# Last rows of w_out and an eighth of one wo group moved to partitions 0 to 31, and O picked in two operations, in a decode block that streams its KV cache

## The chip, the cores and the metric

One core of a Trainium2 chip. The metric is the device time of one execution in microseconds; lower is better. Times inside a profile are counted from the start of its span.

## The reference, cut to what matters

```python
x = A_x                                    # 4 rows of 640, bf16
xn = layernorm(x)
# A: q = xn @ wq (32 heads of 128); attention over k_cache, v_cache (4, 32, 4096, 128); @ wo (4096 x 640)
# B: z = gelu(xn @ w_in); z1 * (w_sp * layernorm(z2) + b_sp) @ w_out (864 x 640)
return x + A(xn) + B(xn)
```

The two caches are 268 MB of the 282 MB that the kernel reads. Each of them is walked in 16 units of 8 MB, named K0 to K15 and V0 to V15; four units, one for each batch row, make a group of eight heads.

## The kernel before

A unit of 128 partitions x 64 KB lies in two of the five slots of one large buffer, so at most two units and a half are there at once. The order is K0 to K3, then V0, K4, V1, K5 and so on. All weights pass through the same five slots.

```python
SL = T * Dh // 2
kv = const.tile([P, 5 * SL], BF16)
def at_slot(i, n, off=0):
    return kv[:, i * SL + off:i * SL + off + n]
...
nc.sync.dma_start(out=w_out[:, 0:FC - 1, :], in_=B_w_out[0:nf, :].rearrange("(p c) n -> p c n", p=P))
nc.sync.dma_start(out=w_out[:FL, FC - 1, :], in_=B_w_out[nf:Fh, :])        # the last 96 rows
...
cuts = {("k", u): (0, T // 2, T) for u in range(NU) if u % B == B - 1}     # K3, K7, K11, K15 in two loads
wo_t = [at_slot((4, 0, 1, 2)[g], HG * NOUT).rearrange("p (c n) -> p c n", c=HG) for g in range(NG)]
...
def emit_K(u, k):                     # eight times for each K unit
    kw = unit(("k", u), t0, t0 + 2 * TC)...
    kT = ktpool.tile([P, 2 * TC * 32], F32, tag="kT", name="kT")          # two buffers
    nc.vector.transpose(kT[:].rearrange("p (t r) -> p t r", r=32), kw)
    ...                               # then 8 matmuls into S
...
# in emit_V: picking O, four operations of 128 elements
nc.vector.tensor_scalar(out=R, in0=O_ps[:, 0, :], scalar1=Mk4[:, 0:1], scalar2=None, op0=ALU.mult)
for c in range(1, 4):
    nc.vector.scalar_tensor_tensor(out=R, in0=O_ps[:, c, :], scalar=Mk4[:, c:c + 1], in1=R, op0=ALU.mult, op1=ALU.add)
...
# in the main loop: the next unit is loaded while this one is computed
load_unit(seq[i + 1])
if key == "k" and u == 2 * B - 1:     # behind both halves of K7
    load_wo(u // B - 1)               # the first wo group, 128 rows of 10 KB, into slot 4
```

Of the kernel before, what the change touches and what calls it, by code (L numbers as in the profile page):

```python
# [16 lines left out]
def kernel(  # L17
# [36 lines left out]
    G = HG * B  # L54
    F2 = B_w_in.shape[1]
    Fh = F2 // 2
    FC = (Fh + P - 1) // P
    FL = Fh - (FC - 1) * P
    NOUT = A_wo.shape[1]
    NH = 2  # L60
    NO2 = NOUT // NH
# [29 lines left out]


    n_q = DC * H * Dh
    wq = at_slot(0, n_q).rearrange("p (c n) -> p c n", c=DC)
    nc.sync.dma_start(out=wq, in_=A_wq.rearrange("(p c) n -> p c n", c=DC))

    ln_t = at_slot(0, 8 * D, n_q)
    x_bf = ln_t[:B, 0:D]
    nc.scalar.dma_start(out=x_bf, in_=x_flat)

    x_res = const.tile([32, NO2], BF16)
    nc.vector.memset(x_res[:], 0.0)

    n_in = DC * F2
    w_in = at_slot(2, n_in).rearrange("p (c f) -> p c f", c=DC)
    nc.sync.dma_start(out=w_in, in_=B_w_in.rearrange("(p c) f -> p c f", c=DC))
    w_out = at_slot(2, FC * NOUT, n_in).rearrange("p (c n) -> p c n", c=FC)

    nf = (FC - 1) * P
    nc.sync.dma_start(out=w_out[:, 0:FC - 1, :], in_=B_w_out[0:nf, :].rearrange("(p c) n -> p c n", p=P))  # L110
    nc.sync.dma_start(out=w_out[:FL, FC - 1, :], in_=B_w_out[nf:Fh, :])  # L111
    sb_bf = const.tile([1, 2], BF16)
    nc.sync.dma_start(out=sb_bf[:, 0:1], in_=B_w_sp)
    nc.sync.dma_start(out=sb_bf[:, 1:2], in_=B_b_sp[None, :])


    seq = [("k", u) for u in range(B)]
# [34 lines left out]

    wo_q = A_wo.rearrange("(g p c) n -> g p c n", p=P, c=HG)
    wo_t = [at_slot((4, 0, 1, 2)[g], HG * NOUT).rearrange("p (c n) -> p c n", c=HG) for g in range(NG)]

    def load_wo(g, c_cuts=(0, HG)):
        for c0, c1 in zip(c_cuts[:-1], c_cuts[1:]):
# [117 lines left out]
    zT_ps = misc_ps([P, 2, FC, B], F32)  # L275
    for part in range(2):
        for fc in range(FC):
            n = P if fc < FC - 1 else FL
            f0 = part * Fh
            for c in range(DC):  # L280
                if fc < FC - 1:
                    w = w_in[:, c, f0:f0 + nf].rearrange("p (f a) -> p a f", a=FC - 1)[:, fc, :]
                else:
                    w = w_in[:, c, f0 + nf:f0 + Fh]
                nc.tensor.matmul(zT_ps[:n, part, fc, :], lhsT=w,
                                 rhs=xnT[:, c, 0:B], start=(c == 0), stop=(c == DC - 1))
    zT = const.tile([P, 2, FC, B], F32)
    nc.vector.memset(zT[:], 0.0)
    uT = const.tile([P, FC, 32], BF16)
    nc.vector.memset(uT[:], 0.0)  # L290
    nc.scalar.activation(out=zT[:, :, 0:FC - 1, :], in_=zT_ps[:, :, 0:FC - 1, :], func=ACT.Gelu_apprx_tanh)
    nc.scalar.activation(out=zT[:FL, :, FC - 1, :], in_=zT_ps[:FL, :, FC - 1, :], func=ACT.Gelu_apprx_tanh)

    one_bf = const.tile([1, P], BF16)
    nc.vector.memset(one_bf[:], 1.0)
# [36 lines left out]


    for fc in range(FC):
        n = P if fc < FC - 1 else FL
        nb = B if fc > 1 else 32
        r0 = 64 * (fc % 2)
        for hf in range(NH):
            nc.tensor.matmul(proj[r0 + 32 * hf:r0 + 32 * hf + nb, 0:NO2], lhsT=uT[:n, fc, 0:nb],
                             rhs=w_out[:n, fc, hf * NO2:(hf + 1) * NO2], start=(fc < 2), stop=False)  # L340


    def fill_qz(g):
# [92 lines left out]
    def emit_V(v):  # L436
        g, b = divmod(v, B)
        O_ps = ps_o.tile([P, 4, Dh], F32, tag="O", name="O")
        vv = unit(("v", v), 0, T)
        for w in range(NW):  # L440
            q = w % 4
            nc.tensor.matmul(O_ps[32 * q:32 * q + 32, :, :], lhsT=Zb[b % 2][:, w].rearrange("p h c -> p (h c)"),  # L442
                             rhs=vv[:, w * 4 * Dh:(w + 1) * 4 * Dh], start=(w < 4), stop=(w >= NW - 4))

        if b == 0:
            R_new = small.tile([P, B, Dh], F32, tag="R", name="R", bufs=1)
            state["R"] = R_new
        R = state["R"][:, b, :]
        nc.vector.tensor_scalar(out=R, in0=O_ps[:, 0, :], scalar1=Mk4[:, 0:1], scalar2=None, op0=ALU.mult)  # L449
        for c in range(1, 4):  # L450
            nc.vector.scalar_tensor_tensor(out=R, in0=O_ps[:, c, :], scalar=Mk4[:, c:c + 1], in1=R, op0=ALU.mult, op1=ALU.add)  # L451
        if b + 2 < B:
            z_fill(g, b + 2)

# [11 lines left out]

    def emit_oT(g):
        om = state.pop(("om", g))[:].rearrange("p h (q c) -> p c h q", c=HG)
        oT_ps = misc_ps([P, HG, B], F32)
        for c in range(HG):  # L470
            nc.tensor.matmul(oT_ps[:, c, :], lhsT=om[:, c, :, :], rhs=B32[:], start=True, stop=True)
        oT = small.tile([P, HG, B], BF16, tag="oT", bufs=3)
        nc.vector.tensor_copy(out=oT[:], in_=oT_ps[:])
        state[("oT", g)] = oT

    def emit_proj(g, cs=range(HG)):
        oT = state[("oT", g)]
        for c in cs:
            for hf in range(NH):
                r0 = 64 * (c % 2) + 32 * hf  # L480
                nc.tensor.matmul(proj[r0:r0 + B, 0:NO2], lhsT=oT[:, c, :],
                                 rhs=wo_t[g][:, c, hf * NO2:(hf + 1) * NO2],
                                 start=False, stop=(g == NG - 2 and c >= HG - 2))

    fill_qz(0)
    for i, item in enumerate(seq):
        if i + 1 < len(seq):
            key, u = seq[i + 1]
            if u == NU - 2 and key == "v":
                x_rows = x_flat.rearrange("b (h n) -> (b h) n", h=NH)  # L490
                for r0, r1 in ((0, 3), (3, 2 * B)):
                    nc.sync.dma_start(out=x_res[4 * r0:4 * r1:4, :], in_=x_rows[r0:r1])
            load_unit(seq[i + 1])
            if key == "k" and u == 2 * B - 1:
                load_wo(u // B - 1)
        else:
            load_wo(NG - 3)
            load_wo(NG - 2)
            load_wo(NG - 1, (0, 4, 6, 7, 8))
        key, u = item  # L500
        g, b = divmod(u, B)
        if key == "k":
            done = b == B - 1 and g > 0
            for k in range(8):
                emit_K(u, k)
                if done and k == 1:
                    emit_sel(g - 1)
                if done and k == 2:
                    emit_oT(g - 1)
                if done and k == 5 and g == 1:  # L510
                    emit_proj(g - 1)
            if b == B - 1:
                if g < NG - 1:
                    fill_qz(g + 1)
                softmax(g)
        else:
            emit_V(u)
            if u == NU - 2:
                for hf in range(NH):
                    nc.tensor.matmul(proj[32 * hf:32 * hf + B, 0:NO2], lhsT=ident_bf[:32, 4 * hf:32:8], rhs=x_res[:],  # L520
                                     start=False, stop=False)
# [10 lines left out]
    oT = state[("oT", NG - 1)]  # L532
    for c in range(HG):

        lhsT = oT[:].rearrange("p c b -> p (c b)") if c == 0 else oT[:, c, :]
        for hf in range(NH):
            nc.tensor.matmul(last[32 * hf:32 * hf + (32 if c == 0 else B), :], lhsT=lhsT,  # L537
                             rhs=wo_t[NG - 1][:, c, hf * NO2:(hf + 1) * NO2], start=(c == 0), stop=(c == HG - 1))
# [33 lines left out]
```

## Time and profile before

| | before |
|---|---|
| median of 3 runs | 665.3 us (664.97 to 665.37) |
| span of the profiled run | 663.5 us |
| main load queue, share of 16 DMA engines' span | 98.8% |
| busiest compute engine | VectorE 54% |
| K7's transposes begin | 247.62 and 257.44 us |
| K8 issued, V5 issued | 266.40, 287.30 us |
| last data landed | 659.93 us |

Three things in the profile carry the argument. The *DMA row* gives the mean busy share of the 16 DMA engines in each fortieth of the span. The *timeline* gives start, duration, engine, line and operation, then in brackets the idle time ahead and what ended it. And for each load the trace keeps its *completion writes*: 16 for a load of 128 rows, three and five for x_res's loads of three and five rows (one mark about 1 us after the issue, which these small loads have besides, is left out). I take each write for one DMA engine, so the engine that is ahead and the one that is behind can be told. The prediction below shows the lines.

### The profile page before, as it was taken

To read this page: it belongs to the slowest core of one execution; us is meant where nothing else is said; L and a number is where in the kernel's file an instruction comes from. 1 tells how busy PE (TensorE), PEld (TensorE's weight loads), DVE (VectorE), ACT (ScalarE), POOL (GpSimd) and SP (SyncE) were. 2 spreads that over 40 slices of the span, in tenths; PEclk is the share of its full clock that TensorE was granted. 3 is DMA by queue.
4 is the path that set the end of the run, shared out by engine and by line. 5 is a ranking of instruction groups with operands and counts; after the bars stand their busy time and mean duration, and the time that the engine had idled before them with its cause. 6 is when DMAs were issued, how large, how long until landed. Compare 5 with 4: busy or idle time off the path is not lost.

```text
span 663.5 us, 5584 instructions
## 1 busy us (share of the span) xinstructions
PE 298.7 (45%) x2366; PEld 111.7 (17%) x2366; DVE 359.9 (54%) x341; ACT 82.6 (12%) x169; POOL 6.2 (1%) x24
## 2 busy tenths in 40 slices
PE   0525765266073457235436075433607244624146
PEld 0401211022021122111112022111202112211012
DVE  5338999656190849509156286745628084940002
ACT  0300000440100000530200000070100000053200
POOL 0000000000000000000000000000000000000000
PEclk9758779678577786667758577865857778756777
DMA  9999999999999999999999999999999999999996
GB/s 368 457 439 420 409 441 440 439 436 436 423 431 440 419 426 448 435 432 423 436 439 432 431 423 438 437 440 435 416 435 436 443 435 412 444 423 436 426 419 248
DMA packets 6949, 282.61 MB, mean 426 GB/s; under 512 B 792, under 2 KB 1164, under 8 KB 1548
## 3 DMA queue, kind: packets, MB, share of 16 engines
q1 hardware_dynamic: 6908, 282.25, 98.8%
q8 instruction: 18, 0.29, 0.2%
q14 instruction: 7, 0.06, 0.0%
q10 hardware_dynamic: 16, 0.01, 0.0%
HBM read 282.25 MB, written 0.01 MB: 425 GB/s over the span
## 4 chain that ended last, share of the span: by engine, by line
DMA 73%; DVE 12%; issue 11%; PE 2%; ACT 1%; SPq 0%; DVEq 0%; ACTq 0%
DMA kv<-in_A_k_cache_dram 65%; DVE kT L360 11%; DMA kv<-in_A_v_cache_dram 4%; DMA kv<-in_A_wo_dram 3%; PE O L442 2%; DVE xd L425 0%; PE last L537 0%; ACT Zb L406 0%; ACT p L414 0%; DVE pT L418 0%; DVE m L378 0%; PE misc L383 0%; PE S L371 0%; SPq L111 0%; ACT xd L425 0%
## 5 line engine op out<-in xcount | busy, mean ns | idle before, releaser
L360 DVE STREAM_TRANSPOSE kT<-kv 128x2048 f32<-128x2048 f32 x128 | 282.8, 2275 | 126.1 <-DMA kv<-in_A_k_cache_dram 126.1
L371 PE MATMUL S<-kT,QZ 128*32 128x512 bf16 x1024 | 192.8, 511 | 230.4 <-DVE kT L360 230.4
L371 PEld LDWEIGHTS <-QZ 128*32 128x32 bf16 x1024 | 61.4, 112 | 355.6 <-issue 336.7
L442 PE MATMUL O<-kv,Zb 128*32 128x512 bf16 x1024 | 76.3, 464 | 59.7 <-ACT Zb L406 30.2
L449 DVE TENSOR_SCALAR R<-O,Mk 128x128 f32<-128x128 f32 x16 | 5.6, 351 | 129.8 <-PE O L442 129.8
L406 ACT ACTIVATE Zb<-xd,MkE 32x256 bf16<-32x256 bf16 x112 | 51.4, 498 | 106.0 <-PE O L442 104.6
L414 ACT ACTIVATE p<-S,negmax 128x512 bf16<-128x512 f32 x8 | 5.4, 683 | 400.4 <-DVE negmax L392 400.4
L442 PEld LDWEIGHTS <-Zb 128*32 128x32 bf16 x1024 | 33.1, 114 | 102.4 <-issue 58.3
L459 PE MATMUL misc<-R,SelR 128*32 128x128 f32 x32 | 6.4, 281 | 26.0 <-DVE R L451 26.0
L425 ACT COPY xd<-pT 32x256 bf16<-32x256 bf16 x28 | 17.2, 613 | 5.7 <-DVE pT L418 5.2
L451 DVE SCALAR_TENSOR_TENSOR R<-O,Mk,R 128x128 f32<-128x128 f32 x48 | 16.8, 351 | 1.7
L425 DVE COPY xd<-pT 32x256 bf16<-32x256 bf16 x36 | 13.1, 364 | 0.6
L346 POOL COPY QZ<-q 32x32 bf16<-32x32 bf16 x16 | 5.1, 321 | 421.6 <-PE S L371 394.8
L418 DVE STREAM_TRANSPOSE pT<-p 128x1024 bf16<-128x1024 bf16 x4 | 5.0, 1245 | 6.3 <-ACT p L414 6.3
L459 PEld LDWEIGHTS misc<-R,SelR 128*32 128x32 f32 x32 | 2.2, 107 | 33.5 <-DVE R L451 24.8
L262 DVE CAST kv<-q 128x512 bf16<-128x512 f32 x4 | 2.5, 684 | 9.4 <-PE q L254 9.4
L378 DVE TENSOR_REDUCE m<-S 128x2 f32<-128x1024 f32 x4 | 4.9, 1225 | 4.9 <-PE S L371 4.9
L383 PE MATMUL misc<-dg,ones_f 128*128 128x256 f32 x8 | 3.7, 558 | 7.6 <-DVE dg L380 7.6
L254 PE MATMUL q<-kv,xnT 128*32 128x512 bf16 x40 | 4.2, 600 | 5.3 <-DMA kv<-in_A_wq_dram 5.3
L462 DVE SCALAR_TENSOR_TENSOR om<-misc,rinv,MkH 32x1024 bf16<-32x1024 f32 x4 | 5.1, 1271 | 2.0 <-PE misc L459 2.0
L430 PE MATMUL misc<-rowsum,SelPe 128*32 128x1 f32 x16 | 2.1, 203 | 9.0 <-ACT p L414 9.0
L191 PE MATMUL misc<-ident_bf,kv 4*128 4x4 bf16 x5 | 0.4, 178 | 10.7 <-DVE kv L187 10.7
(97 smaller groups left out, 70.1 us busy)
## 6 DMA issues: line engine op xcount, KB each, us to landing
kv<-in_A_k_cache_dram SPq DMA_DIRECT2D x8, 4096.0 KB, 29.8
kv<-in_A_v_cache_dram SPq DMA_DIRECT2D x1, 6144.0 KB
kv<-in_A_wq_dram SPq DMA_DIRECT2D x1, 5120.0 KB, 15.6
kv<-in_A_wo_dram SPq DMA_DIRECT2D x3, 1280.0 KB, 20.9
kv<-in_B_w_in_dram SPq DMA_DIRECT2D x1, 2160.0 KB
kv<-in_A_v_cache_dram SPq DMA_DIRECT2D x1, 2048.0 KB
kv<-in_B_w_out_dram SPq DMA_DIRECT2D x1, 960.0 KB
kv<-in_A_wo_dram SPq DMA_DIRECT2D x1, 640.0 KB, 22.4
```

The source lines that it names most:

```text
L346: nc.gpsimd.tensor_copy(out=QZ[r0:r0 + 32, :, :, :, 8 + 8 * hp], in_=q3[r0:r0 + 32, :, NE * hp:NE * hp + NE, g * B:g * B + B].rearrange("p ...
L360: nc.vector.transpose(kT[:].rearrange("p (t r) -> p t r", r=32), kw)
L371: nc.tensor.matmul(S_ps[32 * q:32 * q + 32, e], lhsT=QZ[:, b, 2 * kh + w, e, w0:w0 + 32], rhs=kb[:, i, :, e, :, w], start=(b == 0 and k < ...
L406: nc.scalar.activation(out=dst, in_=src, func=ACT.Copy, scale=mk)
L414: nc.scalar.activation(out=p_bf[:, :, e, :], in_=S_ps[:, e], func=ACT.Exp, bias=negmax[:, e:e + 1], scale=scale, accum_out=rowsum[:, e:e + 1])
L418: nc.vector.transpose(pT[:].rearrange("p t h x -> p (t h x)"), p_bf[:].rearrange("p t e m -> p (t e m)"))
L425: op(out=xd[32 * hp:32 * hp + 32, :, q, :], in_=pT[32 * q:32 * q + 32, :, hp, :].rearrange("p t x -> p x t"))
L442: nc.tensor.matmul(O_ps[32 * q:32 * q + 32, :, :], lhsT=Zb[b % 2][:, w].rearrange("p h c -> p (h c)"), rhs=vv[:, w * 4 * Dh:(w + 1) * 4 * ...
L449: nc.vector.tensor_scalar(out=R, in0=O_ps[:, 0, :], scalar1=Mk4[:, 0:1], scalar2=None, op0=ALU.mult)
L451: nc.vector.scalar_tensor_tensor(out=R, in0=O_ps[:, c, :], scalar=Mk4[:, c:c + 1], in1=R, op0=ALU.mult, op1=ALU.add)
L459: nc.tensor.matmul(oh[:], lhsT=SelR[:, b].rearrange("p h b -> p (h b)"), rhs=state["R"][:, b, :], start=(b == 0), stop=(b == B - 1))
L462: nc.vector.scalar_tensor_tensor(out=om[:], in0=oh[:, None, :].to_broadcast((G, HG, Dh)), scalar=state.pop(("rinv", g))[:, 0:1], in1=MkH[: ...
```

## The change

Its intent is balance among the DMA engines: 96 rows of w_out that did not fill 128 partitions, and the last eighth of the first wo group, are loaded eight rows at a time, which puts them on eight engines; the other eight engines are to be relieved. O is picked in two operations in place of four, and x's residual rows come in one transfer. The core of the diff:

```diff
+    w_rest = ktpool.tile([32, FR, NOUT], BF16, tag="kT", name="w_rest")
+    w_rest_d = B_w_out[nf:Fh, :].rearrange("(i r c) n -> r i c n", r=4, c=FR)
+    for r in range(4):
+        nc.sync.dma_start(out=w_rest[r:32:4], in_=w_rest_d[r])
...
+    GX, CX = 0, HG - 1
+    wo_x = at_slot(4, 4 * NOUT, HG * NOUT)[:32].rearrange("p (q n) -> p q n", q=4)
+    def load_wo_x():
+        src = wo_q[GX].rearrange("(q i r) c n -> r c i q n", q=4, r=4)
+        for r in range(4):
+            nc.sync.dma_start(out=wo_x[r:32:4], in_=src[r, CX])
...
-        nc.vector.tensor_scalar(out=R, in0=O_ps[:, 0, :], scalar1=Mk4[:, 0:1], scalar2=None, op0=ALU.mult)
-        for c in range(1, 4):
-            nc.vector.scalar_tensor_tensor(out=R, in0=O_ps[:, c, :], scalar=Mk4[:, c:c + 1], in1=R, op0=ALU.mult, op1=ALU.add)
+        om4 = ppool.tile([P, 4, Dh], F32, tag="p", name="om4")
+        nc.vector.tensor_tensor(out=om4[:], in0=O_ps[:], in1=Mk4[:, :, None].to_broadcast((P, 4, Dh)), op=ALU.mult)
+        nc.vector.tensor_reduce(out=state["R"][:, b, :], in_=om4[:].rearrange("p c d -> p d c"), axis=AX.X, op=ALU.add)
...
             if key == "k" and u == 2 * B - 1:
-                load_wo(u // B - 1)
+                load_wo(GX, (0, CX))
+                load_wo_x()
```

Cut here: the matmuls that use the new layouts, the x rows in one transfer, and two small loads that moved to another queue.

More of the change, by code (lines that the diff above doesn't have):

```diff
@@ L56 @@
     Fh = F2 // 2
-    FC = (Fh + P - 1) // P
-    FL = Fh - (FC - 1) * P
+    FA = Fh // P
+    FR = (Fh - FA * P) // 32
+    assert Fh == FA * P + FR * 32
+    FC = FA + FR
     NOUT = A_wo.shape[1]
@@ L93 @@
     n_q = DC * H * Dh
-    wq = at_slot(0, n_q).rearrange("p (c n) -> p c n", c=DC)
-    nc.sync.dma_start(out=wq, in_=A_wq.rearrange("(p c) n -> p c n", c=DC))
     ln_t = at_slot(0, 8 * D, n_q)
@@ L99 @@
     nc.scalar.dma_start(out=x_bf, in_=x_flat)
+    sb_bf = const.tile([1, 2], BF16)
+    nc.scalar.dma_start(out=sb_bf[:, 0:1], in_=B_w_sp)
+    nc.scalar.dma_start(out=sb_bf[:, 1:2], in_=B_b_sp[None, :])
     x_res = const.tile([32, NO2], BF16)
     nc.vector.memset(x_res[:], 0.0)
+    wq = at_slot(0, n_q).rearrange("p (c n) -> p c n", c=DC)
+    nc.sync.dma_start(out=wq, in_=A_wq.rearrange("(p c) n -> p c n", c=DC))
     n_in = DC * F2
@@ L106 @@
     nc.sync.dma_start(out=w_in, in_=B_w_in.rearrange("(p c) f -> p c f", c=DC))
-    w_out = at_slot(2, FC * NOUT, n_in).rearrange("p (c n) -> p c n", c=FC)
-    nf = (FC - 1) * P
-    nc.sync.dma_start(out=w_out[:, 0:FC - 1, :], in_=B_w_out[0:nf, :].rearrange("(p c) n -> p c n", p=P))
-    nc.sync.dma_start(out=w_out[:FL, FC - 1, :], in_=B_w_out[nf:Fh, :])
-    sb_bf = const.tile([1, 2], BF16)
-    nc.sync.dma_start(out=sb_bf[:, 0:1], in_=B_w_sp)
-    nc.sync.dma_start(out=sb_bf[:, 1:2], in_=B_b_sp[None, :])
+    nf = FA * P
+    w_out = at_slot(2, FA * NOUT, n_in).rearrange("p (c n) -> p c n", c=FA)
+    nc.sync.dma_start(out=w_out, in_=B_w_out[0:nf, :].rearrange("(p c) n -> p c n", p=P))
+    w_rest = ktpool.tile([32, FR, NOUT], BF16, tag="kT", name="w_rest")
+    w_rest_d = B_w_out[nf:Fh, :].rearrange("(i r c) n -> r i c n", r=4, c=FR)
+    for r in range(4):
+        nc.sync.dma_start(out=w_rest[r:32:4], in_=w_rest_d[r])
     seq = [("k", u) for u in range(B)]
@@ L277 @@
         for fc in range(FC):
-            n = P if fc < FC - 1 else FL
+            n = P if fc < FA else 32
             f0 = part * Fh
             for c in range(DC):
-                if fc < FC - 1:
-                    w = w_in[:, c, f0:f0 + nf].rearrange("p (f a) -> p a f", a=FC - 1)[:, fc, :]
+                if fc < FA:
+                    w = w_in[:, c, f0:f0 + nf].rearrange("p (f a) -> p a f", a=FA)[:, fc, :]
                 else:
-                    w = w_in[:, c, f0 + nf:f0 + Fh]
+                    w = w_in[:, c, f0 + nf:f0 + Fh].rearrange("p (f a) -> p a f", a=FR)[:, fc - FA, :]
                 nc.tensor.matmul(zT_ps[:n, part, fc, :], lhsT=w,
@@ L290 @@
     nc.vector.memset(uT[:], 0.0)
-    nc.scalar.activation(out=zT[:, :, 0:FC - 1, :], in_=zT_ps[:, :, 0:FC - 1, :], func=ACT.Gelu_apprx_tanh)
-    nc.scalar.activation(out=zT[:FL, :, FC - 1, :], in_=zT_ps[:FL, :, FC - 1, :], func=ACT.Gelu_apprx_tanh)
+    nc.scalar.activation(out=zT[:, :, 0:FA, :], in_=zT_ps[:, :, 0:FA, :], func=ACT.Gelu_apprx_tanh)
+    nc.scalar.activation(out=zT[:32, :, FA:FC, :], in_=zT_ps[:32, :, FA:FC, :], func=ACT.Gelu_apprx_tanh)
     one_bf = const.tile([1, P], BF16)
@@ L334 @@
     for fc in range(FC):
-        n = P if fc < FC - 1 else FL
+        n = P if fc < FA else 32
         nb = B if fc > 1 else 32
@@ L339 @@
             nc.tensor.matmul(proj[r0 + 32 * hf:r0 + 32 * hf + nb, 0:NO2], lhsT=uT[:n, fc, 0:nb],
-                             rhs=w_out[:n, fc, hf * NO2:(hf + 1) * NO2], start=(fc < 2), stop=False)
+                             rhs=(w_out[:, fc] if fc < FA else w_rest[:, fc - FA])[:, hf * NO2:(hf + 1) * NO2], start=(fc < 2), stop=False)
     def fill_qz(g):
@@ L447, in emit_V @@
             state["R"] = R_new
-        R = state["R"][:, b, :]
-        nc.vector.tensor_scalar(out=R, in0=O_ps[:, 0, :], scalar1=Mk4[:, 0:1], scalar2=None, op0=ALU.mult)
-        for c in range(1, 4):
-            nc.vector.scalar_tensor_tensor(out=R, in0=O_ps[:, c, :], scalar=Mk4[:, c:c + 1], in1=R, op0=ALU.mult, op1=ALU.add)
+        om4 = ppool.tile([P, 4, Dh], F32, tag="p", name="om4")
+        nc.vector.tensor_tensor(out=om4[:], in0=O_ps[:], in1=Mk4[:, :, None].to_broadcast((P, 4, Dh)), op=ALU.mult)
+        nc.vector.tensor_reduce(out=state["R"][:, b, :], in_=om4[:].rearrange("p c d -> p d c"), axis=AX.X, op=ALU.add)
         if b + 2 < B:
@@ L468, in emit_oT @@
         om = state.pop(("om", g))[:].rearrange("p h (q c) -> p c h q", c=HG)
-        oT_ps = misc_ps([P, HG, B], F32)
-        for c in range(HG):
+        nx = 4 if g == GX else 0
+        oT_ps = misc_ps([P, HG + nx, B], F32)
+        nt = CX if nx else HG
+        for c in range(nt):
             nc.tensor.matmul(oT_ps[:, c, :], lhsT=om[:, c, :, :], rhs=B32[:], start=True, stop=True)
-        oT = small.tile([P, HG, B], BF16, tag="oT", bufs=3)
-        nc.vector.tensor_copy(out=oT[:], in_=oT_ps[:])
+        for x in range(nx):
+            nc.tensor.matmul(oT_ps[:32, HG + x, :], lhsT=om[:, CX, 2 * x:2 * x + 2, :], rhs=B32[:], start=True, stop=True)
+        oT = small.tile([P, HG + 4, B], BF16, tag="oT", bufs=3)
+        nc.vector.tensor_copy(out=oT[:, 0:nt, :], in_=oT_ps[:, 0:nt, :])
+        if nx:
+            nc.vector.tensor_copy(out=oT[:32, HG:, :], in_=oT_ps[:32, HG:, :])
         state[("oT", g)] = oT
@@ L478, in emit_proj @@
         for c in cs:
-            for hf in range(NH):
-                r0 = 64 * (c % 2) + 32 * hf
-                nc.tensor.matmul(proj[r0:r0 + B, 0:NO2], lhsT=oT[:, c, :],
-                                 rhs=wo_t[g][:, c, hf * NO2:(hf + 1) * NO2],
-                                 start=False, stop=(g == NG - 2 and c >= HG - 2))
+            if g == GX and c == CX:
+                parts = [(x % 2, oT[:32, HG + x, :], wo_x[:, x, :]) for x in range(4)]
+            else:
+                parts = [(c % 2, oT[:, c, :], wo_t[g][:, c, :])]
+            for x, (k, lhsT, w) in enumerate(parts):
+                for hf in range(NH):
+                    r0 = 64 * k + 32 * hf
+                    nc.tensor.matmul(proj[r0:r0 + B, 0:NO2], lhsT=lhsT, rhs=w[:, hf * NO2:(hf + 1) * NO2],
+                                     start=False, stop=(g == NG - 2 and c >= HG - 2))
     fill_qz(0)
@@ L489 @@
             if u == NU - 2 and key == "v":
-                x_rows = x_flat.rearrange("b (h n) -> (b h) n", h=NH)
-                for r0, r1 in ((0, 3), (3, 2 * B)):
-                    nc.sync.dma_start(out=x_res[4 * r0:4 * r1:4, :], in_=x_rows[r0:r1])
+                nc.sync.dma_start(out=x_res[0:32:4, :], in_=x_flat.rearrange("b (h n) -> (b h) n", h=NH))
             load_unit(seq[i + 1])
             if key == "k" and u == 2 * B - 1:
-                load_wo(u // B - 1)
+                load_wo(GX, (0, CX))
+                load_wo_x()
         else:
@@ L533 @@
     for c in range(HG):
-        lhsT = oT[:].rearrange("p c b -> p (c b)") if c == 0 else oT[:, c, :]
+        lhsT = oT[:, 0:HG, :].rearrange("p c b -> p (c b)") if c == 0 else oT[:, c, :]
         for hf in range(NH):
```

## The prediction

> **What bounds the kernel now.** I read the engine and slice rows of the page first, then the DMA queues, then the chain in order of time, then the windows of the last microseconds.
>
> ```profile
> PE 298.7 (45%) x2366; PEld 111.7 (17%) x2366; DVE 359.9 (54%) x341; ACT 82.6 (12%) x169; POOL 6.2 (1%) x24
> ...
> DMA  9999999999999999999999999999999999999996
> ...
> q1 hardware_dynamic: 6908, 282.25, 98.8%
> q8 instruction: 18, 0.29, 0.2%
> q14 instruction: 7, 0.06, 0.0%
> ```
>
> No compute engine is above 54%, the DMA engines are at 90% or more in every slice but the last, and q1 alone fills 98.8% of 16 engines' span. 282 MB at some 430 GB/s is the kernel. So only three things move the time: bytes (unchanged here), unevenness among the 16 DMA engines, and moments in which their queues run dry. The windows of the end show the unevenness:
>
> ```profile
> core 0: us, PE busy (x) PEld busy (x) DVE busy (x) ACT busy (x) POOL busy (x), PEclk, DMA share, GB/s
> ...
> 650.00:654.00 4.00, 2.38 (x32) 0.99 (x28) 1.40 (x4) 0.00 (x0) 0.00 (x0) 0.80 0.98 406
> 654.00:656.00 2.00, 1.18 (x23) 0.77 (x23) 1.27 (x1) 0.00 (x0) 0.00 (x0) 1.00 0.87 347
> 656.00:658.00 2.00, 1.08 (x22) 0.74 (x22) 0.63 (x2) 0.00 (x0) 0.00 (x0) 1.00 0.52 200
> 658.00:660.00 2.00, 1.67 (x14) 1.11 (x15) 0.54 (x2) 0.00 (x0) 0.00 (x0) 0.61 0.10 39
> ```
>
> The DMA share (last column but one) fades over 5 us: engines finish one by one. The completion writes that the trace keeps for each load (16 for a load on all engines) say it exactly. After the first's, the last load's come at 0, .28, .37, .59, 1.25, 1.25, 1.29, 2.91, 3.05, 3.06, 3.11, 3.29, 3.38, 3.84, 4.62 and 4.82 us. In the load of wq the spread was 1.4 us; it grows in jumps of 1.5 us at the 16,384-byte packets of q8 (they come in turn to eight engines, two of which get a third) and of 0.7 to 1.0 us at the 8,192-byte packets of q14. The kernel ends with the slowest engine: the last landing is at 659.9, and the last matmuls, the addition and the output take it to 663.5.
>
> The second thing to read is how close the queues come to running dry where the change acts, at the load of the first wo group (timeline, 225 to 305 us):
>
> ```profile
> 231.86 0.33 SPq L158 DMA_DIRECT2D kv<-in_A_wo_dram  x1
> ...
> 241.70 0.33 SPq L150 DMA_DIRECT2D kv<-in_A_v_cache_dram  x1
> ...
> 247.62 8.89 DVE L360 STREAM_TRANSPOSE kT<-kv 128x2048 f32<-128x2048 f32 x4 [1.68 <-DMA kv<-in_A_k_cache_dram]
> ...
> 257.44 8.89 DVE L360 STREAM_TRANSPOSE kT<-kv 128x2048 f32<-128x2048 f32 x4 [0.93 <-DMA kv<-in_A_k_cache_dram]
> ...
> 266.40 0.33 SPq L150 DMA_DIRECT2D kv<-in_A_k_cache_dram  x1
> 267.54 1.23 DVE L378 TENSOR_REDUCE m<-S 128x2 f32<-128x1024 f32 x1 [1.21 <-PE S L371]
> ...
> 280.93 6.32 PE L442 MATMUL O<-kv,Zb 128*32 128x512 bf16 x64 [7.56 <-ACT Zb L406]
> ...
> 287.30 0.33 SPq L150 DMA_DIRECT2D kv<-in_A_v_cache_dram  x1
> ```
>
> Call the units K7 (two halves, the transposes at 247.62 and 257.44), V4 (issued 241.70), K8 (266.40), V5 (287.30). K7's last transpose frees K8's place; K7 is also the last of its group, so softmax and V4's matmuls follow, and only when these end may V5 be issued. V4 has landed on all engines at 279.8 and K8 at 299.1. So the queues have 13 us in hand at K8's issue and 12 us at V5's.
>
> [...] x_res's three and five rows leave three and five completion writes, loads of 96 and 128 rows 16. [...] The trace has 18 such packets for 4763 TensorE records, about one per 265; [...] it costs the DMA engine that carries it 1.5 us. [...]
>
> **The change part by part.**
>
> Balance. Who are the slow engines? [...] I take them for engines 8 to 15. Packets cost 51.5 ns for 1280 bytes (55 ns less 3.5 of overlap), 291 for 7,680, 385 for 10,240; 3,840 bytes are about 144 and 8,960 about 335 by the same line. Rows of w_out: six packets on every engine (309 ns) become four of 3,840 on engines 0 to 7 (578) and none on 8 to 15. wo: 8x381 = 3052 ns becomes 8x335 = 2676, and on 0 to 7 also 16x51.5 = 824. Sum: engines 0 to 7 +0.72 us, 8 to 15 -0.69 us. If nothing else moved, the end would be at lag 4.82-0.69 = 4.13, with the odd engine at 3.84+0.72 = 4.56 or, with one VectorE refill fewer, at 3.6. The gain would be 0.26 to 0.69 us.
>
> Picking O. One TENSOR_SCALAR and three fused ones of 351 ns, 1.50 us with gaps, become one product and one reduction of 512 elements. The reductions take 425 ns for 256 and 1225 for 1024 elements, 1.04 ns per element, so 692 for 512; the product of 256 takes 461, so 728. Sum 1.42 to 1.45 us, perhaps 0.3 more for the strided read. It is neutral; at the end VectorE is done at 656.6, 1.7 us before the last matmuls' weights land. It also saves VectorE 30 instructions of 471, so its fourth refill (after 443) probably falls away.
>
> TensorE and issue. 33 more small matmuls, nearly all at 25 to 34 us, when the queues are full until 42; three more issues on SP and two on ScalarE, all under queued work. Nothing.
>
> What the instruction order shows. I compared the waits of the two built programs. In the changed one the first transpose of K7 waits not for its own half alone but also for the completion of all four eight-row wo loads, which stand behind both halves of K7 in the queue; it is as if the strided rows counted as overlapping with the rest of the large buffer. TensorE, likewise, has the projection with these wo rows ahead of K7's matmuls. So K7's transposes start not at 247.6 but when those loads land. wo landed at 258.35 to 260.40; engines 0 to 7 come 0.72 later, the slowest of them 2.05 behind: 258.35+0.72+2.05 = 261.1. Then eight transposes in a row, 2x8.89 = 17.7: K7 is done at 278.8 instead of 266.3, 12.5 us late. K8 is issued at 278.9; the first load's data came 1.03 us after its issue began, so K8's data start at 279.9. V4's data end at 278.3 to 280.0 on all engines but one: a first hole of up to 1.5 us, and all engines are level at about 279.9. K8 takes 8x2.418 = 19.3, to 299.2. V5 is issued as long after K7's last transpose as before, 287.30-266.34 = 20.96: at 299.8, with data from about 300.7. That is a second hole of 1.5 us.
>
> The cost is counted on the engines that end last. They finished K8's data (0.4 before landing) at about 298.3 before; V5 now starts on all at 300.7: +2.4 us. What was gained by balance lies before the hole and is lost in it. After it the loads, refills and waits are as before, with 10 us in hand again. 665.3+2.4 = 667.7 us.
>
> **The rivals.** (1) Balance alone counts: 664.6 to 665.0. The design speaks for it; against it stand the five waits on K7's first transpose and a reserve of 12 us, almost exactly used up. If the delay is 1.5 us shorter than I reckon, the second hole closes; at about 3 us shorter this rival is right. (2) The slow engines are 0 to 7, so balance is negative: about 666.0 without the hole; with it the same 667.7. [...] (3) The delay is longer, because TensorE's late start or the product's buffer (shared with the softmax) holds transposes or softmax up: each us goes straight to the end, 669 to 670. TensorE needs 1.1 to 1.9 us per transpose of 2.2, which speaks against. (4) The reduction across stride is slow and sets the tail: not before it costs 1 us more.
>
> **Range and chances.** The hole is 20.96+17.7 us of measured steps after a landing known to some 0.5 us, less a reserve known as well; I give it +-0.7, and a fifth to rival 1 and to longer holds together. Prediction 667.7 us, range 666.4 to 668.9. Two per cent is 13 us, beyond any of these: faster 0.005, same 0.985, slower 0.01.
>
> **What would show it.** In the profile after: K7's first transposes at about 261 with an idle time before them some 13 us longer, in one run of eight; K8's issue near 279 and V5's near 300; the DMA share below 0.95 around 280 and 300, nowhere else; the chain that ended last passing through the wo loads of 10 KB a row and a V load. The spread of the last completions should be some 3.5 us, the fast group within 1.5. Wrong would be K7's transposes at 247, or no dip at 300, or an end of data before 660.

How to read it. Its sum came to 665.3 + 2.4 = 667.7 us. Its engine numbers are names only: "0 to 7" are the eight engines of an eight-row load, "8 to 15" the others, here and in the expectations below. That every eight-row load uses the same eight, and that the others are the slow ones, were assumptions of mine; so the +0.72 and -0.69 us of balance, the gain of 0.26 to 0.69 and the 0.72 us in the landing at 261.1 are estimates. The "odd engine" is the one whose last completion comes at 3.84 us. The 18 packets are the 16,384-byte ones of q8, a queue that the profile calls `instruction`; each took 1.02 to 1.10 us, and with the one at 322.7 us the spread of a load's completions rises from 2.06 to 3.49 us, as one engine falls back by 1.5. Of q14's packets of 8,192 bytes, four come when 67, 185, 321 and 443 VectorE instructions have started. By these counts I took q8's packets for TensorE's refills and those four for VectorE's.

## The result, and the profile after

The changed kernel took 669.36 us (median of 6 runs, 667.98 to 670.28) against 665.33 (664.97 to 665.37, 6 runs) of before in the same rounds. The ratio is 1.0059, with a 95% interval of 1.0046 to 1.0072. A ratio here is always the mean time of one kernel's fast runs over that of the other's of the same rounds, so not quite the ratio of the medians. By the 2% measure this is the same time, as predicted. But it is 4.0 us more, not 2.4, and lies 0.5 us outside the predicted range.

The page of the changed kernel, rows as in the prediction:

```profile
DMA  9999999999999999899999999999999999999996
...
q1 hardware_dynamic: 7016, 282.25, 98.4%
q8 instruction: 19, 0.31, 0.2%
q14 instruction: 6, 0.05, 0.0%
```

The kernel is bound as before, but one slice in the middle is no longer full, and it is the slice of 267 to 284 us. (A slice is 16.7 us and a packet up to 2.4, so a hole of 2 us is just visible.) The timeline of the changed kernel in the same stretch:

```profile
233.64 0.33 SPq L172 DMA_DIRECT2D kv<-in_A_wo_dram  x1
...
238.03 2.92 SPq L168 DMA_DIRECT2D kv<-in_A_wo_dram  x4
...
262.31 17.66 DVE L374 STREAM_TRANSPOSE kT<-kv 128x2048 f32<-128x2048 f32 x8 [14.04 <-DMA kv<-in_A_wo_dram]
...
280.00 0.33 SPq L155 DMA_DIRECT2D kv<-in_A_k_cache_dram  x1
...
294.75 5.55 PE L456 MATMUL O<-kv,Zb 128*32 128x512 bf16 x64 [7.57 <-ACT Zb L420]
...
300.35 0.33 SPq L155 DMA_DIRECT2D kv<-in_A_v_cache_dram  x1
```

Read the bracket of K7's transposes: VectorE stood idle for 14.04 us, and what ended it was a load of wo, although the transposes read K7. Before, they began at 247.62. They now run in one set of eight, so K8 is issued at 280.00 in place of 266.40 and V5 at 300.35 in place of 287.30. V4 had landed on the first engine at 277.79 and in the mean at 279.57, and K8's first data came at 281.0: the queue ran dry. The share of the DMA engines between 276 and 306 us (last column but one, GB/s behind it), first before, then after:

```profile
276.00:306.00 30.00, 10.60 (x84) 3.66 (x86) 11.10 (x17) 11.92 (x25) 0.00 (x0) 0.56 1.02 440
```

```profile
276.00:306.00 30.00, 12.45 (x104) 4.54 (x98) 17.74 (x26) 14.98 (x31) 1.26 (x4) 0.71 0.91 378
```

(A packet counts whole where it starts, so a share can be just over 1, and windows of a few us say little.) And the end of the changed kernel:

```profile
656.00:658.00 2.00, 0.52 (x14) 0.50 (x18) 1.47 (x3) 0.00 (x0) 0.00 (x0) 1.00 0.97 404
658.00:660.00 2.00, 1.08 (x21) 0.73 (x13) 1.25 (x2) 0.00 (x0) 0.00 (x0) 1.00 0.99 400
660.00:662.00 2.00, 1.24 (x16) 0.53 (x16) 0.13 (x1) 0.00 (x0) 0.00 (x0) 0.62 0.73 269
662.00:664.00 2.00, 1.70 (x14) 0.99 (x15) 0.97 (x2) 0.00 (x0) 0.00 (x0) 0.52 0.11 41
```

The fade that took 5 us before takes 3.1: the last completion is at 663.85 (659.93 before), the spread 3.11 us (4.82). The holes set the engines level (V4's completions spread over 3.64 us, those of K8 behind the first hole over 0.65), and that gave a part of the loss back.

Where did the time go? The trace's packet records give it as a mean over the 16 engines. I take as the base the first experiment below, which is the same kernel without the holes: its last load completes at 657.15 us in the mean of the 16 engines, and in the changed kernel at 662.03, 4.88 us later.

- First hole, at 277 to 282 us: 2.23 us idle per engine. Second hole, at 301 to 303 us: 0.67 us.
- The first packets behind the holes are slow: a 64 KB packet takes 2418 ns in the stream, but the first ones after K8's issue have a median of 3141 ns, the first after V5's 3055 ns. Over all 16 engines that is 0.62 and 0.56 us. The packets behind them take 2418 again.
- Around 138 to 142 us, long before the part that was changed, 20 packets were slow as well: 0.80 us per engine, 0.65 more than in the base.

The sum is 4.73, of 4.88. The prediction had two holes, of up to 1.5 us each, and nothing of the slow packets, neither those behind the holes nor those at 138 us.

### The profile page after: what moved, and what is told of

The parts are those of the page before. It is cut to its first block, busy times and chain, and to the rows that moved or that the text cites. A ratio compares the mean times of both kernels' runs of the same rounds, so it can differ in the third digit from the quotient of the medians.

```text
span 667.3 us, 5632 instructions
## 1 busy us (share of the span) xinstructions
PE 297.9 (45%) x2399; PEld 111.2 (17%) x2399; DVE 364.5 (55%) x310; ACT 82.6 (12%) x169; POOL 6.2 (1%) x24
## 4 chain that ended last, share of the span: by engine, by line
DMA 63%; DVE 16%; issue 14%; PE 5%; ACT 2%; SPq 0%; DVEq 0%; ACTq 0%
DMA kv<-in_A_k_cache_dram 49%; DVE kT L374 12%; DMA kv<-in_A_wo_dram 7%; DMA kv<-in_A_v_cache_dram 5%; PE O L456 3%; DMA kv<-in_A_wq_dram 2%; DVE xd L439 1%; ACT Zb L420 1%; PE S L385 1%; ACT p L428 1%; DVE pT L432 1%; DVE m L392 1%; PE misc L397 0%; SPq L168 0%; PE last L559 0%
## 5 line engine op out<-in xcount | busy, mean ns | idle before, releaser
L385 PE MATMUL S<-kT,QZ 128*32 128x512 bf16 x1024 | 187.8, 500 | 213.5 <-DVE kT L374 213.5
L463 DVE TENSOR_TENSOR om<-O,Mk 128x512 f32<-128x512 f32 x16 | 11.1, 691 | 133.5 <-PE O L456 133.5
L464 DVE TENSOR_REDUCE R<-om 128x128 f32<-128x512 f32 x16 | 16.3, 1018 | 0.5
L505 PE MATMUL proj<-kv,oT 128*4 128x320 bf16 (+1 forms) x54 | 3.8, 410 | 14.7 <-DMA kv<-in_A_wo_dram 14.7
```

The costliest lines, as they stand in the source:

```text
L385: nc.tensor.matmul(S_ps[32 * q:32 * q + 32, e], lhsT=QZ[:, b, 2 * kh + w, e, w0:w0 + 32], rhs=kb[:, i, :, e, :, w], start=(b == 0 and k < ...
L463: nc.vector.tensor_tensor(out=om4[:], in0=O_ps[:], in1=Mk4[:, :, None].to_broadcast((P, 4, Dh)), op=ALU.mult)
L464: nc.vector.tensor_reduce(out=state["R"][:, b, :], in_=om4[:].rearrange("p c d -> p d c"), axis=AX.X, op=ALU.add)
```

## The experiments

Twelve runs were made, three of them repeats, in three sets of four, each timed in five rounds against the kernel before (665.29, 665.21 and 665.09 us, 9 runs each).

### 1. The eight-row wo in a buffer of its own

Theory: the loss is the wait of K7's transposes for loads that have nothing to do with them. Rival: the moved rows cost by themselves.

```diff
-    wo_x = at_slot(4, 4 * NOUT, HG * NOUT)[:32].rearrange("p (q n) -> p q n", q=4)
+    wo_x = const.tile([32, 4, NOUT], BF16, name="wo_x")
```

(To make room, one pool has two buffers in place of three and two small tiles at the end moved into it.)

> The changed kernel with the eighth of wo in a buffer of its own (to make room the product pool has two buffers instead of three and the output rows lie in it); then no transpose of K7 waits for these loads. Theory (the wait makes two holes in the DMA queues, the rows moved between engines gain a little): K7's first transpose at about 248 us, no hole near 280 and 300, 664.6 to 665.1 us. Rival A (eight-row loads, the added small matmuls or the picking in two operations cost time by themselves): stays at 668 to 670. Rival B (engines 0 to 7 are the slow ones, so the moved rows cost): about 666.

Measured: 665.02 us (664.83 to 666.08), ratio 0.9999 (0.9986 to 1.0012). The timeline:

```profile
247.63 8.89 DVE L374 STREAM_TRANSPOSE kT<-kv 128x2048 f32<-128x2048 f32 x4 [1.14 <-DMA kv<-in_A_k_cache_dram]
...
266.42 0.33 SPq L155 DMA_DIRECT2D kv<-in_A_k_cache_dram  x1
...
287.08 0.33 SPq L155 DMA_DIRECT2D kv<-in_A_v_cache_dram  x1
```

With every part of the change in place and, apart from the room made for it, only the address of wo_x altered, K7, K8 and V5 are where they were before, and the loss is gone. The whole 4 us is what the wait brings about, and the rival falls. It is also the direct sign that the wait was a false one: the transposes need nothing of wo_x.

### 2. The kernel before with the wait alone

```diff
         kT = ktpool.tile([P, 2 * TC * 32], F32, tag="kT", name="kT")
+        if u == 2 * B - 1 and k == 0:
+            nc.vector.tensor_copy(out=kT[:, 0:1], in_=wo_t[0][:, HG - 1, NOUT - 1:NOUT])
```

The copied element is overwritten by the transpose; the result stays right.

> The kernel before with one thing added: a copy of one element per partition of the first wo group into the buffer of K7's first transpose, so that this transpose waits for the wo load. No row is moved. Theory: K7's transposes start near 260.6 (the landing of wo) and end near 278.4, K8 is issued there, V5 20.4 to 21 us later, at 299; data a microsecond later and a slow first packet: 667.3 to 668.5 us, a little less than the changed kernel because the wait ends 1.7 us earlier. Rival A (the wait is covered by the 12 us of reserve): 665.3.

Measured: 669.48 us (668.8 to 671.45), ratio 1.0067 (1.0053 to 1.008).

```profile
260.40 4.49 DVE L362 STREAM_TRANSPOSE kT<-kv 128x2048 f32<-128x2048 f32 x2
260.44 1.24 PE L483 MATMUL proj<-kv,oT 128*4 128x320 bf16 x16 [14.84 <-DMA kv<-in_A_wo_dram]
264.94 3.60 PE L373 MATMUL S<-kT,QZ 128*32 128x512 bf16 x16 [3.27 <-DVE kT L362]
266.87 13.28 DVE L362 STREAM_TRANSPOSE kT<-kv 128x2048 f32<-128x2048 f32 x6 [1.98 <-PE S L373]
...
280.18 0.33 SPq L150 DMA_DIRECT2D kv<-in_A_k_cache_dram  x1
...
301.73 0.33 SPq L150 DMA_DIRECT2D kv<-in_A_v_cache_dram  x1
```

Without a row moved, holding K7's transposes makes a loss of this size. The expectation was 1 us low for a reason that the brackets show: the third transpose waited another 1.98 us for its buffer, because TensorE began K7's matmuls only at 264.94, when the second transpose was done (264.89). It was not the projection with wo that held them: this was over at 261.7, and TensorE then stood idle for 3.27 us. In the two kernels with an added copy (this one and experiment 5) the first matmuls start at the end of the second transpose, in all the others at the end of the first, so this wait came with the copy; why is not shown. That the loss equals that of the changed kernel is thus luck in part: here wo landed 1.8 us earlier than the eight-row loads did there, and the copy added 2.0. By the slope of the table below, the hold without the 2.0 would have made some 668.5 to 669 us (an estimate).

### 3. The changed kernel with the first wo group loaded whole

```diff
-    GX, CX = 0, HG - 1
+    GX, CX = -1, HG - 1
...
-                load_wo(GX, (0, CX))
-                load_wo_x()
+                load_wo(u // B - 1)
```

> The changed kernel with the first wo group loaded whole as before; the last rows of w_out in their own buffer, the merged load of x_res and the picking in two operations stay. Theory: the wait is gone and only the small part of the balance is left (engines 0 to 7 +0.27 us, 8 to 15 -0.31): 664.8 to 665.2 us, K7's first transpose near 248. Rival A (the other parts cost time): 666 to 669.

Measured: 664.74 us (664.63 to 665.35), ratio 0.9991 (0.9979 to 1.0004). K8 is issued at 266.30 and V5 at 285.60. The other parts, w_out's rows, x and the pick, cost nothing that can be measured.

### 4. The eight rows to eight neighbouring partitions

```diff
-        src = wo_q[GX].rearrange("(q i r) c n -> r c i q n", q=4, r=4)
+        src = wo_q[GX].rearrange("(q r i) c n -> r c i q n", q=4, r=4)
-            nc.sync.dma_start(out=wo_x[r:32:4], in_=src[r, CX])
+            nc.sync.dma_start(out=wo_x[8 * r:8 * r + 8], in_=src[r, CX])
```

> The changed kernel with the eight rows of each wo load in eight partitions that follow each other (rows to partitions 8r to 8r+7) instead of every fourth. The built program then has no wait of K7's transposes for these loads. Theory: no hole, 664.6 to 665.1 us as with the own buffer, if writing eight neighbouring partitions is as quick. Rival C [...] 665.5 to 667. If the wait is not the cause: 669.

Measured: 666.62 us (665.78 to 667.49), ratio 1.0018 (1.0004 to 1.0031). K7's transposes start at 247.71 and 257.52, so the false wait comes from the stride over partitions: with the rows side by side in the same large buffer it isn't there. K8 is issued at 270.60, because its load waited for the projection with wo (4.1 us); that lies inside the reserve, and no engine runs idle. But this version has a cost of its own. The 1280-byte packets take 75 ns in the median (55 in the changed kernel), and V4's packets beside them are slow too. Over the mean times of their sizes, the packets of 250 to 268 us lose 0.69 us (64 KB), 0.22 (8,960 bytes) and 0.16 (1280 bytes) per engine, 1.07 in all, where the run with its own buffer loses 0.06. That is about the 1.2 us of the ratio. Why they are slower is not shown: the edit changes both the partitions that are written and the rows of wo that a load reads, and the packet records don't name the engine. (Rival C was that loads to neighbouring partitions take longer.)

### 5. The same wait, 2.8 us shorter

To find how much delay the reserve takes: the kernel before, K7's first transpose held until K7's own second half has landed.

```diff
+        if u == 2 * B - 1 and k == 0:
+            nc.vector.tensor_copy(out=kT[:, 0:1], in_=at_slot(3, 1, SL - 1))
```

> The kernel before, with K7's first transpose held (by a copy of one element per partition, whose result is overwritten) until K7's own second half has landed, at 257.3 us in the trace of before. No row is moved. That is the same hold as in the changed kernel, but 2.8 us shorter: K8 issued at about 275.2, V5 at about 296.1 us; V4's data end on the first engine at 277.3 and K8's at 296.7. So no queue runs empty before the next load is issued. Theory 'reserve' (as in the prediction: only time with an empty queue costs, 1.0 us of start included): 665.3 to 665.6 us, no step in the completions after 297 us. Theory 'restart' (formed from the traces of after and of the wait-alone run: a load issued less than some 2.4 us before the queue runs out has slow first packets too, 0.6 us each): most of the first 16 packets of V5 take about 3.0 us in place of 2.42, the mean completion after it is 0.4 to 0.7 us later, and the time is 665.7 to 666.2 us. Theory 'every us of delay costs': about 668 us.

Measured: 667.39 us (665.63 to 668.02), ratio 1.0026 (1.0013 to 1.0038). The dose came out larger than planned: as in experiment 2 the third transpose waited for TensorE (1.98 us), K8 was issued at 278.48 in place of 275.2 and V5 at 298.60 in place of 296.1. The extra 1.98 us is again the copy's: the first matmuls start at 263.25, after the second transpose (263.19). So the queue did run dry (1.08 and 0.32 us per engine), and this doesn't tell 'reserve' from 'restart' by the time, which lies nearest to the third theory; experiment 12 decides on that one. It gives another point of the dose, and the same slow packets: 3127 ns in the median after K8's issue. Around 138 us this run also has 19 slow packets; V1 was issued at 136.68 there, 0.6 us later than in before.

### 6. The two-operation pick alone

```diff
-        nc.vector.tensor_scalar(...)          # and three scalar_tensor_tensor
+        nc.vector.tensor_tensor(out=om4[:], ...)
+        nc.vector.tensor_reduce(out=state["R"][:, b, :], ...)
```

> The kernel before with O picked in two operations and nothing else changed. If the two operations lie beside other work, as the prediction says, 665.0 to 665.6 us (the same), with the sum 1.7 us per unit in place of 1.5; at most 0.7 us either way from VectorE's instruction refills, one fewer of which is possible. If the longer picking delays the V loads that wait behind it or the end, up to +0.2 us per V unit of the last group, below 1 us in all.

Measured: 665.29 us (664.92 to 665.48), ratio 0.9999 (0.9986 to 1.0013). The groups of instructions of this run:

```profile
L450 DVE TENSOR_REDUCE R<-om 128x128 f32<-128x512 f32 x16 | 16.7, 1044 | 0.5
L449 DVE TENSOR_TENSOR om<-O,Mk 128x512 f32<-128x512 f32 x16 | 11.1, 692 | 126.5 <-PE O L442 126.5
```

The product takes 692 ns and the reduction 1044, so 1.74 us in place of 1.50. The forecast of the sum, 1.42 to 1.45 us plus perhaps 0.3 for the strided read, was right with its reserve. The reduction, whose elements lie 512 bytes apart, took about 2 ns per element, where the other reductions take 1.04 by the prediction's figures. It is off the path: VectorE waits 126.5 us in all for the matmuls ahead of it.

### 7. and 8. Is what is left faster? The third kernel again, and the same with the old pick

The edit of the second of them is the reverse of that of experiment 6, in the kernel of experiment 3.

> The changed kernel with the first wo group loaded whole, a second time, to see whether it beats the kernel before: 664.74 in the first set, ratio 0.9991 with an interval that held 1. If its rest (last rows of w_out, x_res in one transfer) balances the engines: 664.5 to 665.0 and an upper end of the interval at or below 1.000. If the 0.5 us was chance: 665.2 to 665.5.

> The same with O picked in four operations as before: only the w_out rows and the single x_res transfer are left of the change. If the pick is neutral, as in its own run (665.29), this equals e3_again within 0.4 us. If the fewer VectorE instructions of the two-operation pick save an instruction refill on the engine that ends last, this is 0.5 to 1.0 us slower than e3_again.

Measured: 664.77 us (664.56 to 665.17), ratio 0.9997 (0.9984 to 1.0009), and 664.88 us (664.4 to 665.69), ratio 0.9998 (0.9985 to 1.0012). Both medians are below that of before, 665.09, but neither interval leaves out 1. No version here is shown to be faster than the kernel before, and the pick makes no difference.

### 9. More bytes for the eight engines of the eight-row loads

```diff
+    more = A_k_cache[0, 0:HG].rearrange("e (m t) d -> (e m) (t d)", t=T)
+    for j in range(2):
+        more_t = ktpool.tile([32, 4096], BF16, tag="kT", name=f"more{j}")
+        for r in range(4):
+            nc.sync.dma_start(out=more_t[r:32:4], in_=more[8 * r:8 * r + 8, 4096 * j:4096 * j + 4096])
     load_unit(seq[0])
```

> The kernel before with eight more loads of eight rows of 8 KB (into a scratch buffer that nothing reads) ahead of the first K unit, so engines 0 to 7 carry about 2.4 us more each and engines 8 to 15 nothing; x_res is loaded as eight rows in one transfer, so that its completion writes show where engines 0 to 7 stand at 612 us. If engines 0 to 7 are the fast ones (as the prediction took them), the end moves by 0 to 0.5 us: 665.3 to 665.8 us, and x_res's completions lie among the whole spread. If some of the slowest engines are among 0 to 7, the end moves by most of 2.4 us: 667.0 to 667.8 us, and the last completion of x_res is the last of all by about 2 us.

Measured: 671.25 us (670.63 to 671.41, 4 runs), ratio 1.0088 (1.0074 to 1.0101): beyond both expectations, and the fault is that of the experiment. The timeline shows the queue's issues:

```profile
16.27 10.21 SPq L164 DMA_DIRECT2D more<-in_A_k_cache_dram  x6
...
26.53 1.80 SPq L150 DMA_DIRECT2D kv<-in_A_k_cache_dram  x2
```

Six of the eight small issues took 10.2 us, K units behind them came late, and the first of these completed at 47.9 us in place of 42.3, with all engines within 0.5 us: an early hole (3.7 us idle per engine from 22 to 32 us, none in before). So the time says nothing on balance. The completion writes do say something. The one x_res load of eight rows ends at 616.66 us; the load on all engines just before it ends at 616.48. So the slowest engine is one of x_res's eight here. It is so in experiment 1 as well (610.80 and 610.71). In the changed kernel it is not (614.40 and 615.52). If x_res's eight are the same engines in each kernel, which the traces don't show, the slowest engine is thus not in a fixed half of them.

### 10. and 11. The changed kernel twice more

No edit.

> The changed kernel once more, unaltered, for a second profile. In the first one the granted TensorE clock was 0.50 from 118 to 124 us (1.00 in before), the softmax of the first group took 1.2 us longer, V1 was issued only 1.3 us before the queue ran out, and 20 packets around 138 to 142 us were slow: all engines lost 0.66 us there. If that was chance, the second profile has no such step at 138 us and its last landing is 663.0 to 663.4 us, with the two holes as before (K8 issued at 279.0 to 280.0 us); if it belongs to the change, the step is there again. Time 668.5 to 670 us either way.

> The changed kernel a third time, for the spread from run to run. The first six runs lay at 668.0 to 670.3, the next five at 667.2 to 668.8 us; the two profiles differ in the issue of K8 (280.00 and 278.82) and of V5 (300.35 and 298.29). If the loss is the two holes, and a hole's length changes with the wo landing and with TensorE's speed in the softmax and O-matmuls between the issues, the median lies between 667 and 670 us, the runs spread over 1.5 us or more while those of before stay within 1.1, and the profiled run's excess over 665.3 follows its V5 issue: +2.4 at 298.3, +4.0 at 300.35, so about 1 us per us. If the time does not follow the V5 issue (off by over 0.8 us), the holes are not the whole loss.

Measured: 667.6 us (667.15 to 668.75), ratio 1.0037 (1.0025 to 1.005), and 668.87 us (667.03 to 669.54), ratio 1.0055 (1.0043 to 1.0068). The first did not reach the 668.5 that I expected. With the first result, these are 16 runs of one program: 667.03 to 670.28, median 668.75. The 27 runs of before in the three sets lie between 664.82 and 666.44. So the change made the time 3.5 us longer in the median, and its runs span 3.2 us where those of before span 1.6.

The step at 138 us is small in both (0.2 us per engine), so it does not belong to the change, and in the first profile it was chance: V1 was issued only 1.3 us before the first engine ran out of data there, at a TensorE clock of 0.50 through the softmax ahead of it.

What differs in the second hole is TensorE. The stretch from K7's last transpose to V5's issue contains the softmax and 64 matmuls. Windows of 281 to 284 us in these two runs, the one of 667.6 us first; the columns are the busy times of PE, weight loads, VectorE, ScalarE and GpSimd, then the granted TensorE clock (as a share of full speed), the DMA share and GB/s:

```profile
281.00:284.00 3.00, 0.67 (x2) 0.30 (x2) 1.49 (x5) 0.46 (x1) 0.47 (x2) 0.80 0.81 350
```

```profile
281.00:284.00 3.00, 1.19 (x2) 0.50 (x2) 1.46 (x5) 0.00 (x0) 0.45 (x2) 0.50 0.81 350
```

The same two matmuls take 0.67 us at a granted clock of 0.80 and 1.19 at 0.50. The O-matmuls take 5.36 and 5.91. V5 is issued at 298.29 and 299.33, and the second hole is 0.00 and 0.66 us per engine. The clock records put the fall to 0.50 at 282.77 us in the first and at 280.94 in the second, after and before the two matmuls at 281.9. What makes the clock fall, and at another moment from run to run, is not shown.

### 12. The order of the loads

```diff
-            load_unit(seq[i + 1])
             if key == "k" and u == 2 * B - 1:
+                load_unit(seq[i + 1], (0, T // 2))
                 load_wo(GX, (0, CX))
                 load_wo_x()
+                load_unit(seq[i + 1], (T // 2, T))
+            else:
+                load_unit(seq[i + 1])
```

> The changed kernel with the order of four loads altered: K7's first half, then the wo rows (whole and eight-row loads), then K7's second half. All its parts are kept, wo_x still lies in the big buffer, and K7's first transpose still waits for the eight-row loads, but these now land at about 251 us and K7's second half at about 261, so K7 is done at about 270 and K8 issued at 270 in place of 280, V5 at about 290.5. That is 3.6 us later than before and well within the reserve of 12. If only the lost reserve costs: 664.7 to 665.6 us, no hole at 277 or 301. If the wait costs by itself, or the rows do: 666 us or more.

Measured: 665.05 us (664.68 to 666.01), ratio 1.0002 (0.9989 to 1.0014).

```profile
251.45 8.89 DVE L374 STREAM_TRANSPOSE kT<-kv 128x2048 f32<-128x2048 f32 x4 [3.27 <-DMA kv<-in_A_wo_dram]
...
269.99 0.33 SPq L155 DMA_DIRECT2D kv<-in_A_k_cache_dram  x1
...
290.31 0.33 SPq L155 DMA_DIRECT2D kv<-in_A_v_cache_dram  x1
```

The false wait is still there, in the bracket, but it is 3.27 us and lies inside the reserve. K8 and V5 are 3.6 and 3.0 us later than before, and that costs nothing: no idle engine, no slow packet at 277 or 301 us. So it isn't a wait that costs, nor a late issue, but only an issue that comes after the reserve is used up.

### The dose

The kernel before, and all profiled runs in which K7 was held, in the order of V5's issue. Idle is the time per engine in the two holes together (some 0.07 us of it are gaps between packets that are there without a hole too); the next column is the mean of the last load's completions; the time is that of the profiled run itself.

| run | K8 issued | V5 issued | idle | mean last completion | time |
|---|---|---|---|---|---|
| before | 266.40 | 287.30 | 0.07 | 657.43 | 665.23 |
| order (12) | 269.99 | 290.31 | 0.06 | 657.13 | 665.33 |
| changed, again (10) | 278.82 | 298.29 | 1.66 | 659.79 | 667.15 |
| shorter wait (5) | 278.48 | 298.60 | 1.40 | 660.27 | 667.50 |
| changed, third (11) | 278.79 | 299.33 | 2.58 | 660.72 | 668.75 |
| changed | 280.00 | 300.35 | 2.90 | 662.03 | 669.46 |
| wait alone (2) | 280.18 | 301.73 | 4.48 | 663.08 | 670.44 |

Up to 290.3 nothing is lost. From 298.3 to 301.7 the time grows by 3.29 us for 3.44 us of V5's issue: nearly 1 us per us.

## Why the prediction was right or wrong

- **The mechanism: right.** The false wait, read from the order of instructions, is there, and experiments 1, 2 and 12 show that the loss comes of it, and only once it uses up the reserve. The two holes are where they were foretold, and the chain that ended last passes through the wo loads.
- **K7's transposes: right to 0.1 us, in two of three profiles.** The wo rows were to land at 261.1, K7 to be done at 278.8 and K8 to be issued at 278.9. The second and third profile have 260.9, 278.8 and 278.8. The first has 262.1, 280.0 and 280.0; there the eight engines were 0.6 us later in the mean (the step at 138 us), and the slowest of them was another 0.65 behind. The first hole was longer than foretold ("up to 1.5 us"): 1.6 to 2.2 us per engine in the mean of all. V4's data were to end at 278.3 us or later on all engines but one; in the second profile they end earlier on nine (completions less the 0.4). That does not enter the forecast, for K8 starts behind the hole on all engines.
- **The step that failed: "V5 now starts on all at 300.7: +2.4 us", and behind it "After it the loads, refills and waits are as before".** Two terms of this sum were mis-sized. First, the restart. I counted 1.0 us from an issue to its first data, which was right (0.95 to 1.02 in the profiles with holes), but full speed from there. The first packet of each engine behind a hole takes about 3.1 us in place of 2.42, so a hole costs 0.55 to 0.73 us per engine in addition to its length. In the third profile V5 was issued at 299.33, half a us before the forecast of 299.8, and its first packets began at 300.67 in the mean, as forecast; but V5 landed at 321.12 in place of 320.5, and the last completions were 3.29 us later than before in the mean: the 0.67 us of V5's first packets is the greater part of what the forecast lacked. Second, "V5 is issued as long after K7's last transpose as before", 20.96 us. It was 20.4, 19.5 and 20.6 us, because the stretch runs at a clock that differs from run to run (0.80 and 0.50 from 281 to 284 us in the second and third). I took it from one trace as a fixed step, and gave the whole hole +-0.7; the 2 us between the earliest and the latest V5 issue did not fit into that.
- **In numbers, for the first result:** V5 was to land at 300.7 + 19.35 + 0.4 = 320.5 us, and landed at 322.17 in the mean. Of the 1.7 us, 0.55 are the later issue, 0.56 are slow first packets, and most of the rest is K8 still under way on some engines: V5's first packets start 1.49 us after the issue in the mean of the engines, 0.52 later than the first of them. The loss given back at the end, since the spread fell from 4.82 to 3.11 us, was foretold ("some 3.5 us").
- **Balance: wrong, but without effect.** I took the eight engines that an eight-row load leaves out for the slow ones; no trace showed it. By the completion writes the slowest engine is among x_res's eight in experiments 1 and 9 and outside them in the changed kernel. Rid of the holes, the change gains nothing that can be measured (0.9999, 1.0002). The forecast had said that any gain would be lost in the hole; that it would be 0.26 to 0.69 us otherwise was not borne out.
- **Rival 3 came nearest to the time** ("each us goes straight to the end, 669 to 670"), and the slope of nearly 1 in the dose agrees, but its reasons were others than those found in the changed kernel: TensorE did not hold up the transposes there (it did in the wait-alone run, behind the added copy), and the product's buffer held nothing. Rival 1 falls by the result. Rival 2 falls by experiment 1: rid of the holes, the moved rows cost nothing. Rival 4 falls by experiment 6.
- **Range and chances.** Same within 2% was right. The time was 0.5 us above the range in its first set and inside it in the two others (667.6 and 668.87). That is not to be read as luck alone: the middle of all 16 runs, 668.75, is 1.05 us above the forecast, about the size of the restart that was left out with a little of the clock.

What stays open: why the first packets behind a hole are slow, and at how short a lead (the time from a load's issue to the end of the data ahead of it on the first engine) the effect begins. At V1's issue, before 138 us, 64 KB packets of over 2.5 us number 1 or 2 in three profiles at leads of 2.6 to 3.1 us, 1 to 10 in eight at 1.9 to 2.5, and 19 and 20 in two at 1.9 and 1.3 (experiment 9 left out), so the lead alone does not tell. And whether the changed kernel's spread from run to run is the clock alone; two profiles show it, 16 runs are too few to say that nothing else is in it.

## What to carry to other kernels

When a kernel is bound by a stream of loads, look for the time between the issue of a load and the end of the data queued ahead of it: that reserve is what a new wait may use up for nothing, and beyond it each us cost nearly one here, the slow first packets (some 0.6 us per hole) included. Before moving a small load into a large shared buffer, look in the built program at which instructions now wait for it: rows with a stride over partitions counted here as overlapping with K7's unit; a buffer of its own removed the wait, and an earlier place in the queue made it harmless. And once the reserve is gone, the time inherits every variation of the engines that trigger the loads, so give such a forecast a wider range than the kernel before shows.
